# GLU tiles of a fused backward pass: an order on VectorE changed, one product a step later, and another buffer for the modulation sums

## The chip, the core and the metric

The kernel runs on one core of one Trainium2 chip. The time is the device time of one execution in microseconds (us). Before the change the median of three runs is 3124.64 us (3122.74 to 3125.85). One more execution was profiled: it took 3127.18 us, and its span, from the first to the last instruction, is 3125.4 us.

## What is computed

A block with layer norms and modulation (shift, scale and gate rows made from a condition `c`) holds a recurrent attention and a gated unit (GLU). The kernel returns the output of the block and the gradients for all its inputs. The part that is changed is the GLU, forward and backward, with the layer norm in front of it:

```python
# x is the attention's result with its residual; g, u are 1792 wide, the rest is 512 wide
h = layernorm(x) * (1 + cb) + sb
g = h @ w_gate;  u = h @ w_up
hh = sigmoid(g) * u
b = hh @ w_down
out = x + gb * b
# reference: jax.vjp of the whole block; the gradients of sb, cb, gb and ga are sums over all 2048 rows
```

## The kernel before

The stage (`phase3`) treats 2048 rows in 16 tiles of 128 rows. Each tile goes through seven steps, `s0` to `s6`, and `run_pipeline` works one step of seven different tiles in each iteration, the deepest step first. In iteration `it` the tile `j` of step `k` is `it - k`, so there are 22 iterations: the first ones fill the pipeline, iterations 6 to 15 hold all seven steps, and from iteration 16 on `s0` is gone, from 18 on `s2`, and so on.

- `s0` (layer norm): `t0 = a_rows*ga`, `x1 = t0 + x0`, statistics, `rstd` and `db = dout*gb` on GpSimd (called POOL in the profile), `xhf`, `h2a`, `h2`, and the stores of `db` and `h2`.
- `s1`: two DMA transposes on the SyncE queue, into `hdT`.
- `s2`: eight products of 128x448 on TensorE, gate and up in turn, taken out of PSUM by ScalarE as `sg` and `u`. Then `hh = sg*u` on VectorE, its store, and `umh = u - hh` on POOL.
- `s3`: four products of 128x448 (`dp`). VectorE multiplies each by `sg` into a quarter of `du` (L1064), and then makes `dg = du*umh` (L1065). POOL issues the stores DUROWS and DGROWS.
- `s4`: `hhT @ w_down` into one PSUM tile, copied to `b_bf` by ScalarE. VectorE makes `t1 = b_bf*gb` (L1084), POOL `o_sb = t1 + x1` (L1086) and the store of the output (L1087). VectorE makes `pr = dout*b_bf` (L1089), a product that `s6` sums over the rows.
- `s5`: 28 products into one PSUM tile (`hp`, L1099). ScalarE copies it (`dh2b`), VectorE makes `dxh` (L1106), `pr2` (L1109), `junk` with a sum (L1112), `bb`, `cc`, `ta`, and `dx1` (L1124). Then come the store DX1ROWS, `da = dx1*ga` on VectorE (L1127), the store DAROWS, and `pr3 = dx1*a_rows` on POOL (L1130, `pr_ga` in the profile).
- `s6`: four products with ones sum `pr3`, `dh2b`, `pr2` and `pr` into `acc_ps`, and `da` is transposed on TensorE.

PSUM tiles of the stage come from one pool of five (`psM`). In one iteration they are taken in the order `hp`, `bp`, four `dp`, then gate and up eight times. So the first up product can only be written when the first quarter of `du` has read the first `dp`, the second gate product when the second quarter has read its `dp`, and so on.

The order of each engine's instructions is fixed when the kernel is built, by a scheduler that works from the program's order and its own estimate of times; each engine then works its list strictly in order and waits for semaphores. On VectorE a full iteration has this order before the change: `hh` of the iteration before, `dxh`, `pr2`, `junk`, `bb`, `cc`, `ta`, `dx1`, `t1`, `da`, `pr`, four `du`, `t0`, `dg`, `x1`, statistics, `xhf`, `h2a`, `h2`, `hh`. On POOL: `umh`, DX1ROWS, `pr_ga`, DAROWS, `o_sb`, output store, DUROWS, DGROWS, `rstd`, `db`, DBROWS, H2ROWS, HHROWS, `umh`.

After the loop the four modulation sums are copied from `acc_ps` to a tile `accs` of the stage's pool `sbp` (L1184), and POOL issues four small DMAs from it to DMOD (L1186). Then the pools of the stage close. The next part computes the gradients of the weights (L1164, L1234) and, mixed in, turns attention weights for the following stage: TensorE transposes into two PSUM tiles `wtp`, and VectorE (two of three) or ScalarE (one of three) copies them to `WoT`, which lies where the closed pools were. The ScalarE queue also issues a 2 MB load of the rows `h2` into the buffer `Wk` (L1222), from element 8192 to 16384 of each partition; in the instruction list it stands ahead of ScalarE's first copy to `WoT`.

Of the kernel before, what the change touches and what calls it, by code (L numbers as in the profile page):

```python
# [7 lines left out]
BF16 = mybir.dt.bfloat16  # L8
F32 = mybir.dt.float32
AF = mybir.ActivationFunctionType  # L10
ALU = mybir.AluOpType
# [29 lines left out]
class K:  # L41
# [879 lines left out]
    def phase3(self):  # L921
        nc, tc, cfg, io = self.nc, self.tc, self.cfg, self.io
        D, DC, F, FC, NT, T = cfg.D, cfg.DC, cfg.F, cfg.FC, cfg.NT, cfg.T
# [4 lines left out]
        out_rows = io["out_0"].rearrange("o s d -> (o s) d")  # L928
        nseg = 128 // T
        d = self.dram  # L930
        with ExitStack() as ctx:
# [4 lines left out]
            sbp = ctx.enter_context(tc.tile_pool(name="p3s", bufs=2, reuse_waits="tile"))  # L936
            w_gate, w_up, w_down, w_gateT, w_upT = self.w_gate, self.w_up, self.w_down, self.w_gateT, self.w_upT
            w_downT = wtp.tile([128, DC, F], BF16, name="w_downT")
            ga_bc, sb_bc, cb1_bc, gb_bc = (self.bcs[i] for i in (2, 3, 4, 5))
# [8 lines left out]
            def mm():  # L948
                return psM.tile([128, 512], F32, name="mm", tag="m")
# [78 lines left out]
            def s2(j, st):  # L1028
# [19 lines left out]
                st.update(sg=sg, hh=hh, umh=umh)  # L1048
                return st

            def s3(j, st):
                r0, r1 = j * 128, (j + 1) * 128
                sg, umh, hdT = st["sg"], st["umh"], st["hdT"]
                hhT = sbp.tile([128, FC, 128], BF16, name="hhT", bufs=1)
                nc.sync.dma_start(hhT[:], st["hh"][:], transpose=True)
                du = sbp.tile([128, F], BF16, name="du", bufs=2)
                dg = sbp.tile([128, F], BF16, name="dg", bufs=2)
                for ch in range(NCH):
                    sl = slice(ch * CH, (ch + 1) * CH)
                    dp = mm()  # L1060
                    for c in range(DC):
                        nc.tensor.matmul(dp[:, 0:CH], lhsT=hdT[:, DC + c, :], rhs=w_downT[:, c, sl],
                                         start=(c == 0), stop=(c == DC - 1))
                    nc.vector.tensor_tensor(du[:, sl], dp[:, 0:CH], sg[:, sl], op=ALU.mult)  # L1064
                nc.vector.tensor_tensor(dg[:], du[:], umh[:], op=ALU.mult)  # L1065
                nc.gpsimd.dma_start(self.DUROWS[r0:r1, :], du[:])
                nc.gpsimd.dma_start(self.DGROWS[r0:r1, :], dg[:])
                st.update(hhT=hhT, du=du, dg=dg)
                return st

            def s4(j, st):
                r0, r1 = j * 128, (j + 1) * 128
                hhT = st["hhT"]
                bp = mm()
                for fc in range(FC):
                    nc.tensor.matmul(bp[:], lhsT=hhT[:, fc, :], rhs=w_down[:, fc, :], start=(fc == 0), stop=(fc == FC - 1))
                duT = sbp.tile([128, FC, 128], BF16, name="duT", bufs=1)
                dgT = sbp.tile([128, FC, 128], BF16, name="dgT", bufs=1)
                nc.sync.dma_start(duT[:], st["du"][:], transpose=True)
                nc.sync.dma_start(dgT[:], st["dg"][:], transpose=True)  # L1080
                b_bf = sbp.tile([128, D], BF16, name="b_bf", bufs=2)
                nc.scalar.activation(b_bf[:], bp[:], AF.Copy)
                t1 = sbp.tile([128, D], F32, name="t1", tag="f32tmp", bufs=5)
                nc.vector.tensor_tensor(t1[:], b_bf[:], gb_bc[:], op=ALU.mult)  # L1084
                o_sb = sbp.tile([128, D], BF16, name="o_sb", bufs=2)
                nc.gpsimd.tensor_tensor(o_sb[:], t1[:], st["x1"][:], op=ALU.add)  # L1086
                nc.gpsimd.dma_start(out_rows[r0:r1, :], o_sb[:])  # L1087
                pr = sbp.tile([128, D], BF16, name="pr_gb", bufs=3)
                nc.vector.tensor_tensor(pr[:], st["dout"][:], b_bf[:], op=ALU.mult)  # L1089
                st.update(duT=duT, dgT=dgT, pr=pr)  # L1090
                return st

            def s5(j, st):
                r0, r1 = j * 128, (j + 1) * 128
                hp = mm()
                n = 0
                for (xT, wT) in ((st["duT"], w_upT), (st["dgT"], w_gateT)):
                    for fc in range(FC):
                        nc.tensor.matmul(hp[:], lhsT=xT[:, fc, :], rhs=wT[:, fc, :], start=(n == 0), stop=(n == 2 * FC - 1))  # L1099
                        n += 1  # L1100
                xh2, rstd, dout, a_rows = st["xh2"], st["rstd"], st["dout"], st["a_rows"]
                dh2b = sbp.tile([128, D], BF16, name="dh2b", bufs=1)
                nc.scalar.activation(dh2b[:], hp[:], AF.Copy)
                dxh = sbp.tile([128, D], F32, name="dxh", tag="f32tmp", bufs=5)
                s1_ = sbp.tile([128, 1], F32, name="s1", bufs=2)
                nc.vector.scalar_tensor_tensor(out=dxh[:], in0=hp[:], scalar=1.0, in1=cb1_bc[:], op0=ALU.mult, op1=ALU.mult,  # L1106
                                               accum_out=s1_[:])
                pr2 = sbp.tile([128, D], BF16, name="pr_cb", bufs=1)
                nc.vector.tensor_tensor(pr2[:], hp[:], xh2[:], op=ALU.mult)  # L1109
                junk = sbp.tile([128, D], F32, name="junk", tag="f32tmp", bufs=5)  # L1110
                s2_ = sbp.tile([128, 1], F32, name="s2", bufs=2)
                nc.vector.scalar_tensor_tensor(out=junk[:], in0=dxh[:], scalar=1.0, in1=xh2[:], op0=ALU.mult, op1=ALU.mult,  # L1112
                                               accum_out=s2_[:])
                bb = sbp.tile([128, 1], F32, name="bb", bufs=2)
                cc = sbp.tile([128, 1], F32, name="cc", bufs=2)
                nc.vector.tensor_scalar(bb[:], s1_[:], rstd[:, 0:1], -1.0 / D, op0=ALU.mult, op1=ALU.mult)
                nc.vector.tensor_scalar(cc[:], s2_[:], rstd[:, 0:1], -1.0 / D, op0=ALU.mult, op1=ALU.mult)
                ta = sbp.tile([128, D], F32, name="ta", tag="f32tmp", bufs=5)
                nc.vector.scalar_tensor_tensor(out=ta[:], in0=dxh[:], scalar=rstd[:, 0:1], in1=dout[:], op0=ALU.mult,
                                               op1=ALU.add)  # L1120
                tb = sbp.tile([128, D], F32, name="tb", tag="f32tmp", bufs=5)
                nc.scalar.activation(tb[:], xh2[:], AF.Identity, scale=cc[:, 0:1], bias=bb[:, 0:1])
                dx1 = sbp.tile([128, D], F32, name="dx1", bufs=1)
                nc.vector.tensor_tensor(dx1[:], ta[:], tb[:], op=ALU.add)  # L1124
                nc.gpsimd.dma_start(self.DX1ROWS[r0:r1, :], dx1[:])
                da = sbp.tile([128, D], BF16, name="da", bufs=2)
                nc.vector.tensor_tensor(da[:], dx1[:], ga_bc[:], op=ALU.mult)  # L1127
                nc.gpsimd.dma_start(self.DAROWS[r0:r1, :], da[:])
                pr3 = sbp.tile([128, D], BF16, name="pr_ga", bufs=1)
                nc.gpsimd.tensor_tensor(pr3[:], dx1[:], a_rows[:], op=ALU.mult)  # L1130
                st.update(dh2b=dh2b, pr2=pr2, pr3=pr3, da=da)
                return st

            def s6(j, st):
# [23 lines left out]
            def load_hr(g):  # L1158
                w = min(384, F - 384 * g)
                (nc.sync if g < 2 else nc.scalar).dma_start(hrs[g][:, :, 0:w], self.HHROWS[:, 384 * g:384 * g + w].rearrange("(j p) f -> p j f", p=128))  # L1160
# [9 lines left out]
            def after(it):  # L1170
                if it == NT + 1:
                    nc.scalar.dma_start(dbr, self.DBROWS[:, :].rearrange("(j p) d -> p j d", p=128))
                elif it == NT + 2:
                    load_hr(0)
                elif NT + 3 <= it < NT + 6:
                    if it == NT + 3:
                        load_hr(1)
                    wd_chunk(it - NT - 3, mm(), sbp.tile([128, D], BF16, name="ot2", tag="db", bufs=2))

            self.run_pipeline(NT, [s0, s1, s2, s3, s4, s5, s6], deepest_first=True, after=after)  # L1180
            ET = mybir.EngineType
            self.pin_behind(i0, self.pinned, [ET.DVE, ET.Activation, ET.Pool])
            accs = sbp.tile([128, D], F32, name="accs", bufs=1)
            nc.vector.tensor_copy(accs[:], acc_ps[:, :])  # L1184
            for i in range(4):
                nc.gpsimd.dma_start(self.DMOD[2 + i:3 + i, :], accs[32 * i:32 * i + 1, :])  # L1186
# [906 lines left out]
```

The softmax here doesn't subtract the row's maximum and nothing guards it: scores larger than these inputs give would overflow.

## Time and profile before

| what | value |
|---|---|
| median of three runs | 3124.64 us |
| profiled execution / its span | 3127.18 us / 3125.4 us |
| TensorE busy, all of the span | 3004.2 us (96%) |
| VectorE, ScalarE, POOL busy | 1616.2, 1264.6, 1473.0 us |
| GLU tiles, iterations 4 to 21 | about 1060 to 1380 us of the span |
| one iteration, first six full ones | 20.13 us |
| one iteration, the next ones | 19.70 us |
| TensorE's idle time at L1043 in the stage | 16.3 us in 15 waits |
| mean granted TensorE clock | 0.989 |

The lengths of an iteration are the distances of the `da` product from one iteration to the next: it starts at 1085.45, 1105.58, 1125.71, 1145.84, 1165.97, 1186.11, 1206.24 us and then every 19.70 us. The same product takes 2.07 us in the first six of these and 0.69 us in the other ones. The page's times are those of one execution; a wait is put down to the event that came last.

### The profile page before, as it was taken

Reading aid. Unit: us, or ns where it says so; the run is one execution under the profiler, and the core shown is the slowest. Engines: PE = TensorE matmul, PEld = TensorE weight load, DVE = VectorE, ACT = ScalarE, POOL = GpSimd, SP = SyncE. Lnnn points to the kernel's source line nnn. Section 1 sums busy time; section 2 is a strip of 40 time slices with the busy share of each in tenths; the row PEclk is TensorE's granted clock in tenths of the full one; section 3 lists DMA queues with packets and bytes.
Section 4 is the critical chain, followed back from the end, with each engine's and each line's share of the span. In section 5 each row is a group of like instructions: output and inputs, shape, how many; then the busy total and the mean of one; then the engine's idle time right before and its main releaser. Section 6 shows DMA issues by size and latency. Waiting matters only on the chain.

```text
span 3125.4 us, 106126 instructions
## 1 busy us (share of the span) xinstructions
PE 3004.2 (96%) x43769; PEld 1838.1 (59%) x43845; DVE 1616.2 (52%) x3738; ACT 1264.6 (40%) x3053; POOL 1473.0 (47%) x2974
## 2 busy tenths in 40 slices
PE   5999999999998799989989999999999999999999
PEld 3666666666665444445567777777777754455454
DVE  4556656655654777733255555555655542322321
ACT  2555555555554433322155555555555530110111
POOL 3666666666665466531144444444444432233322
PEclk8999999999999899999999999999999999999999
DMA  8887788788787798898589999999999998666674
GB/s 295 214 214 199 205 214 212 204 207 213 205 207 237 177 214 219 202 267 271 185 218 244 240 248 242 244 243 248 244 239 244 243 270 285 201 202 213 196 234 147
DMA packets 844665, 703.54 MB, mean 225 GB/s; under 512 B 543794, under 2 KB 716370, under 8 KB 843796
## 3 DMA queue, kind: packets, MB, share of 16 engines
q1 hardware_dynamic: 714404, 486.69, 62.2%
q0 software_dynamic: 59120, 148.64, 14.6%
q10 hardware_dynamic: 70656, 61.41, 6.3%
q8 instruction: 345, 5.65, 0.8%
q14 instruction: 140, 1.15, 0.1%
HBM read 294.93 MB, written 276.35 MB: 183 GB/s over the span
## 4 chain that ended last, share of the span: by engine, by line
PE 50%; issue 4%; DMA 2%; POOL 1%; DVE 0%; SPq 0%; ACT 0%; POOLq 0%; DVEq 0%
PE gps L1885 10%; PE dh_ps L216 8%; PE g_ps L1547 6%; PE pass_ps L256 5%; PE gps5o L1899 4%; PE dhq_ps L224 4%; PE gps L1234 3%; PE dh_tps L216 3%; PE dp_ps L1526 2%; PE tps L1459 2%; PE dp_ps L1534 1%; PE turn_ps L1413 1%; PE dh_ft L321 1%; PE gps L1164 1%; PE wtp L1300 1%
## 5 line engine op out<-in xcount | busy, mean ns | idle before, releaser
L1885 PE MATMUL gps<-rows,hrows 128*128 128x512 bf16 (+2 forms) x2124 | 415.6, 355 | 1.9
L1885 PEld LDWEIGHTS <-hrows 128*128 128x128 bf16 x2160 | 211.2, 98 | 204.6
L256 PEld LDWEIGHTS <-hT 128*32 128x32 bf16 x6144 | 158.2, 97 | 161.3 <-issue 1.9
L1591 POOL COPY dOst<-RAd 96x512 bf16<-96x512 bf16 x128 | 75.4, 613 | 311.3 <-DVE RAd L63 311.1
L1889 POOL DMA_DIRECT2D out_dram<-ot x108 | 81.4, 754 | 258.6 <-DVE ot L63 132.3
L63 DVE CAST ot<-gps 128x512 bf16<-128x512 f32 (+3 forms) x76 | 48.1, 633 | 284.9 <-PE gps L1885 191.6
L875 POOL TENSOR_TENSOR Pst<-Pst,rden 120x1408 bf16<-120x1408 bf16 x63 | 159.6, 2533 | 57.4 <-issue 38.9
L61 ACT ACTIVATE ot<-gps 128x512 bf16<-128x512 f32 (+3 forms) x75 | 41.3, 551 | 356.2 <-PE gps L1885 225.3
L61 ACT ACTIVATE dVT<-g_ps 128x512 bf16<-128x512 f32 (+1 forms) x192 | 109.3, 569 | 95.9 <-PE g_ps L1547 95.5
L63 DVE CAST RA0v<-pass_ps 128x512 bf16<-128x512 f32 x128 | 88.5, 692 | 89.5 <-PE pass_ps L256 86.2
L216 PE MATMUL dh_ps<-WvT,dVT 128*32 128x512 bf16 x2048 | 133.4, 380 | 0.0
L256 PE MATMUL pass_ps<-Wv,hT 128*32 128x512 bf16 x2048 | 133.3, 380 | 0.0
L1899 PE MATMUL gps5o<-WoT,rows 128*128 128x512 bf16 x580 | 127.8, 379 | 1.0 <-DMA rows<-OSR 0.3
L224 PE MATMUL at_ps<-Wo,OT 128*32 128x256 bf16 x4096 | 125.0, 275 | 0.1
L256 PE MATMUL pass_ps<-Wk,hT 128*32 128x512 bf16 x2048 | 123.3, 383 | 1.5 <-ACT hT L865 1.1
L1536 DVE SCALAR_TENSOR_TENSOR dS<-dp_ps,Pst_l 128x512 bf16<-128x512 f32 (+1 forms) x192 | 112.0, 639 | 22.8 <-PE dp_ps L1534 22.8
L256 PE MATMUL pass_ps<-WoT,dyT 128*32 128x256 bf16 (+1 forms) x3072 | 122.4, 308 | 0.9 <-ACT dyT L1665 0.9
L224 PE MATMUL dhq_ps<-WqT,dQT 128*32 128x256 bf16 x4096 | 122.9, 273 | 0.0
L216 PE MATMUL dh_ps<-WkT,dKT 128*32 128x512 bf16 x2048 | 122.3, 380 | 0.0
L256 PE MATMUL pass_ps<-Wq,hT 128*32 128x512 bf16 x2048 | 121.6, 379 | 0.0
L224 PEld LDWEIGHTS <-dQT 128*32 128x32 bf16 x4096 | 109.6, 97 | 15.9
L709 ACT ACTIVATE ET<-st_ps 128x480 bf16<-128x480 f32 (+1 forms) x192 | 96.1, 535 | 42.6 <-ACT qT L61 34.7
(419 smaller groups left out, 7164.5 us busy)
## 6 DMA issues: line engine op xcount, KB each, us to landing
OSR<-Ost SPq DMA_DIRECT2D x64, 352.0 KB
OT<-OT SPq DMA_DIRECT2D x64, 352.0 KB
VT<-VTr SPq DMA_DIRECT2D x64, 352.0 KB
PS<-Pst SPq DMA_DIRECT2D x64, 352.0 KB
OT_l<-OT SPq DMA_DIRECT2D x64, 352.0 KB
Pst_l<-PS SPq DMA_DIRECT2D x64, 352.0 KB
VT_l<-VT SPq DMA_DIRECT2D x64, 352.0 KB
DVR<-rows_x POOLq DMA_DIRECT2D x64, 352.0 KB, 6.4
```

The costliest lines, as they stand in the source:

```text
L61: return nc.scalar.activation(out, in_, AF.Copy)
L63: return nc.vector.tensor_copy(out, in_)
L216: self.nc.tensor.matmul(ps[32 * j:32 * j + 32, :], lhsT=lhsT, rhs=w, start=(n < 4), stop=(n >= total - 4), tile_position=(0, 32 * j))
L224: nc.tensor.matmul(ps[32 * j:32 * j + 32, :], lhsT=x[k], rhs=w[k][:, 256 * d:256 * d + 256], start=(n == 0), stop=(n == total - 1), tile_p ...
L256: self.nc.tensor.matmul(ps[32 * j:32 * j + 32, :], lhsT=lhs(c), rhs=rhs, start=(c == 0), stop=(c == DC - 1), tile_position=(0, 32 * j))
L709: nc.scalar.activation(part3(ET, pi)[:, 0:n, 0:120], st_ps[:, 0:n, 0:120], AF.Exp, scale=cfg.scale)
L875: nc.gpsimd.tensor_tensor(Pst[0:120, :, :], Pst[0:120, :, :], rden[:, :].unsqueeze(2).to_broadcast([120, G, 128]), op=ALU.mult)
L1234: nc.tensor.matmul(ps[:], lhsT=h2r[:, j, c * 128:(c + 1) * 128], rhs=xr[:, j, :], start=(j == 0), stop=(j == NT - 1))
L1536: nc.vector.scalar_tensor_tensor(out=part3(dS, pi), in0=ps[:, 0:n, :], scalar=cfg.scale, in1=part3(Pst, pi), op0=ALU.mult, op1=ALU.mult)
L1547: nc.tensor.matmul(ps[:, j, :], lhsT=lh[:, g * GW:(g + 1) * GW], rhs=rh[:, g * GW:(g + 1) * GW], start=True, stop=True)
L1885: nc.tensor.matmul(ps[:, 0:ng * E], lhsT=hrows[:, tp_, c * 128:(c + 1) * 128], rhs=rows[:, tp_, 0:ng * E], start=(tp_ == 0), stop=(tp_ == ...
L1899: nc.tensor.matmul(pss[gg][:], lhsT=src[0][:, src[1], gg * E:(gg + 1) * E], rhs=dyrows[:, tp_, :], start=(tp_ == order[0]), stop=(tp_ == o ...
```

## The change

`s3` runs all its VectorE work on `dp` first and then calls `flush`, which works off a list of things put aside: the output's product with its sum and store (from `s4`), and the product `da` with its store (from `s5`). `after` calls `flush` too, for iterations without `s3`. The product `pr` is written in `s5` and not in `s4`, with two buffers instead of three. The sums go to a region of the weight buffer `Wk` (elements 14336 to 15360 of each partition) and not to a tile of the stage's pool.

```diff
+            late = []
+            def flush():
+                while late:
+                    late.pop(0)()
 ...
             def s3(j, st):
 ...
                     nc.vector.tensor_tensor(du[:, sl], dp[:, 0:CH], sg[:, sl], op=ALU.mult)
+                flush()
                 nc.vector.tensor_tensor(dg[:], du[:], umh[:], op=ALU.mult)
 ...
             def s4(j, st):
 ...
-                t1 = sbp.tile([128, D], F32, name="t1", tag="f32tmp", bufs=5)
-                nc.vector.tensor_tensor(t1[:], b_bf[:], gb_bc[:], op=ALU.mult)
-                o_sb = sbp.tile([128, D], BF16, name="o_sb", bufs=2)
-                nc.gpsimd.tensor_tensor(o_sb[:], t1[:], st["x1"][:], op=ALU.add)
-                nc.gpsimd.dma_start(out_rows[r0:r1, :], o_sb[:])
-                pr = sbp.tile([128, D], BF16, name="pr_gb", bufs=3)
-                nc.vector.tensor_tensor(pr[:], st["dout"][:], b_bf[:], op=ALU.mult)
-                st.update(duT=duT, dgT=dgT, pr=pr)
+                def out():
+                    t1 = sbp.tile([128, D], F32, name="t1", tag="f32tmp", bufs=5)
+                    nc.vector.tensor_tensor(t1[:], b_bf[:], gb_bc[:], op=ALU.mult)
+                    o_sb = sbp.tile([128, D], BF16, name="o_sb", bufs=2)
+                    nc.gpsimd.tensor_tensor(o_sb[:], t1[:], st["x1"][:], op=ALU.add)
+                    nc.gpsimd.dma_start(out_rows[r0:r1, :], o_sb[:])
+                late.append(out)
+                st.update(duT=duT, dgT=dgT, b_bf=b_bf)
 ...
             def s5(j, st):
 ...
+                pr = sbp.tile([128, D], BF16, name="pr_gb", bufs=2)
+                nc.vector.tensor_tensor(pr[:], dout[:], st["b_bf"][:], op=ALU.mult)
 ...
-                nc.vector.tensor_tensor(da[:], dx1[:], ga_bc[:], op=ALU.mult)
-                nc.gpsimd.dma_start(self.DAROWS[r0:r1, :], da[:])
+                def out():
+                    nc.vector.tensor_tensor(da[:], dx1[:], ga_bc[:], op=ALU.mult)
+                    nc.gpsimd.dma_start(self.DAROWS[r0:r1, :], da[:])
+                late.append(out)
 ...
+            later = after
+            def after(it):
+                flush()
+                later(it)
 ...
-            accs = sbp.tile([128, D], F32, name="accs", bufs=1)
+            accs = self.flat(self.Wk, 2 * DC * F, 2 * D, F32)
```

The scheduler turns this into the following order of a full iteration. VectorE: `hh` of the iteration before, `dxh`, `pr2`, `junk`, `bb`, `cc`, `ta`, `dx1`, `du`, `du`, `da`, `du`, `du`, `t1`, `dg`, `t0`, `pr`, `x1`, and the rest as before. The product `pr` is brought forward over the end of the iteration, so that it stands in the same iteration as before, only later. POOL: `umh`, DX1ROWS, `pr_ga`, DAROWS, DUROWS, `o_sb`, DGROWS, output store, `rstd`, and the rest as before. TensorE's, ScalarE's and SyncE's orders within the stage stay. In iteration 4 VectorE's order is `t1`, `du`, `du`, `t0`, `du`, `du`, `x1`, `dg`, where it was `t1`, `pr`, four `du`, `t0`, `dg`, `x1`. In the last iteration POOL's `pr_ga` comes ahead of DAROWS. After the loop, VectorE's first copy to `WoT` no longer waits for the DMAs to DMOD, and the load of the `h2` rows on ScalarE's queue now waits for all four of them.

More of the change, by code (lines that the diff above doesn't have):

```diff
@@ L1126, in s5 @@
                 da = sbp.tile([128, D], BF16, name="da", bufs=2)
-                nc.vector.tensor_tensor(da[:], dx1[:], ga_bc[:], op=ALU.mult)
-                nc.gpsimd.dma_start(self.DAROWS[r0:r1, :], da[:])
+                def out():
+                    nc.vector.tensor_tensor(da[:], dx1[:], ga_bc[:], op=ALU.mult)
+                    nc.gpsimd.dma_start(self.DAROWS[r0:r1, :], da[:])
+                late.append(out)
                 pr3 = sbp.tile([128, D], BF16, name="pr_ga", bufs=1)
                 nc.gpsimd.tensor_tensor(pr3[:], dx1[:], a_rows[:], op=ALU.mult)
-                st.update(dh2b=dh2b, pr2=pr2, pr3=pr3, da=da)
+                st.update(dh2b=dh2b, pr2=pr2, pr3=pr3, da=da, pr=pr)
                 return st
```

## The prediction

> **What bounds the kernel now.** First the totals: TensorE is busy for 96% of the span. So I looked for the places in the stage where TensorE stands still, in the list of waits between 1040 and 1385 us, and then read what happens there from the timeline.
>
> ```profile
> PE mm L1043 <- DVE du L1064: 16.3, 15, 3.4
> DVE dxh L1106 <- ACT dh2b L1103: 57.1, 16, 5.7
> ```
>
> The first line is all that TensorE loses inside the loop: 15 waits for `du`, 16.3 us. The second seems to say that VectorE has some 3.5 us to spare in each iteration. The timeline of one iteration shows both, and why the second is deceptive:
>
> ```profile
> 1179.21 3.59 POOL L1047 TENSOR_TENSOR umh<-u,hh 128x1792 bf16<-128x1792 bf16 x1
> 1183.02 0.68 DVE L1112 SCALAR_TENSOR_TENSOR junk<-dxh,xh 128x512 f32<-128x512 f32 x1
> 1186.11 2.07 DVE L1127 TENSOR_TENSOR da<-dx,Wv 128x512 bf16<-128x512 f32 x1
> 1186.45 1.17 POOL L1130 TENSOR_TENSOR pr_ga<-dx,Wv 128x512 bf16<-128x512 f32 x1
> 1188.10 0.41 DVE L1089 TENSOR_TENSOR pr_gb<-Wq,b_bf 128x512 bf16<-128x512 bf16 x1
> 1188.44 2.21 DVE L1064 TENSOR_TENSOR du<-mm,sg 128x448 bf16<-128x448 f32 x4
> 1189.10 0.92 PE L1043 MATMUL mm<-Wk,hdT 128*128 128x448 bf16 x4 [1.17 <-DVE du L1064]
> ```
>
> TensorE waits 1.17 us because `du` stands behind `t1`, `da` and `pr`. `da` needs 2.07 us here and 0.69 us where it gets by: it stood still until POOL's `pr_ga` ended (1187.62) and was done 0.56 later. VectorE products of two SBUF tiles and POOL's products shut each other out. `du` (one input in PSUM) is never slowed: 0.60 to 0.61 us in all 64. Look at `junk`: it starts 0.22 after `umh` ends. It has two SBUF inputs, so it could not have started sooner. Two more places show the size of it:
>
> ```profile
> 1061.58 5.31 DVE L1089 TENSOR_TENSOR pr_gb<-Wv,b_bf 128x512 bf16<-128x512 bf16 x1
> 1061.80 3.58 POOL L1047 TENSOR_TENSOR umh<-u,hh 128x1792 bf16<-128x1792 bf16 x1
> 1065.33 1.26 POOL L1086 TENSOR_TENSOR o_sb<-t,x 128x512 bf16<-128x512 f32 x1
> ...
> L1926 DVE SCALAR_TENSOR_TENSOR dx_junk<-dx_dxh,xh x16: 681/1524/1531, 2608.4 to 2992.7; 128x512 f32<-128x512 f32 x16
> ```
>
> `pr` (0.41 alone) sat out `umh` and `o_sb` together; in the last stage the same form as `junk` takes 1.52 instead of 0.68 where POOL is ahead. Behind the loop, the chain of waits and the timeline show the sums' way out:
>
> ```profile
> 1382.11 6.04 DMA DMOD<-accs
> ...
> 1388.71 0.76 DVE L63 COPY WoT<-wtp 128x512 bf16<-128x512 bf16 x2 [4.44 <-DMA DMOD<-accs]
> 1389.19 1.01 PE L1313 MATMUL wtp<-ident,stage 128*128 128x128 bf16 x8 [4.34 <-DVE WoT L63]
> ```
>
> TensorE waits 4.34 us for a copy that waits for four 2 KB DMAs, and then runs at half clock until 1396 (eight transposes 1.01 us, where they take 0.61 at 1395.84).
>
> **The change, part by part.** I take the profiled execution as it is; its span is 0.8 above the median of the runs, so I take the difference off 3124.64.
>
> *Full iterations.* Time 0 is 1185.51, where the operation after `dx1` starts. Now two `du` go first (0.53 each), and `da` comes to 1.06. `pr_ga` runs from 0.94 to 2.11, so `da` is always late and the next operation starts at 2.59 (as before: 0.48 after `pr_ga`). Two `du`: 3.65. `t1` 0.60: `dg` starts at 4.25. On POOL, DAROWS waits for `da`, DUROWS for the last `du` (3.73, plus the 0.29 that every store waits after its tile): 4.03 to 4.58. `o_sb` waits for `t1`, whose record ends at 4.34. So `dg` has the port first, until 5.33; `o_sb`, waiting, gets it next, as `pr_ga` did ahead of `pr` in the ten faster iterations (there `da` ended at 1206.93, `pr_ga` 1.01 later), and ends at about 6.4. `t0` stands behind it, the next operation starts at 6.9, `pr` takes 0.34, and `x1` starts at 7.24. Before, it was 1192.17 - 1185.51 = 6.66, or 6.23 in the faster iterations. From `x1` to the end of `hh` nothing changes (6.32): 13.56. `umh` ends 4.45 after `hh` (1198.49 to 1202.94): 18.01. If `junk` is there by then it ends 0.55 later, 18.56, and from the end of `junk` to time 0 it is 1.81 (1183.70 to 1185.51). This ring of VectorE and POOL is 20.37 us long. Before it was 12.98 + 4.45 + 0.55 + 1.81 = 19.79 with the slow `da` and some 19.4 with the fast one, below the 20.13 and 19.70 that ran, so it did not show. Is `junk` there? The first up product starts 0.1 after the first `du`, at 0.7; `hp` ends 12.2 later (1189.10 to 1201.30), `dxh` 0.63 after that, `junk` at 14.7: well ahead of 18.0. So the ring decides. TensorE alone would need 20.13 - 1.17 = 18.96, and goes on waiting for `du`, 1.4 us each time. Eleven such iterations (5 to 15): 11 x 20.37 = 224.1 against 6 x 20.13 + 5 x 19.70 = 219.3: **+4.8**.
>
> *Way out.* In iteration 16 the first `du` comes 2.5 sooner after `dx1` (at 0 and not behind `t1`, `da` and `pr`): **-2.5**. `s0` is gone there, `hh` comes early, `umh` is over before `junk`, so iteration 17 is TensorE's alone: **-0.7** (19.70 - 18.96).
>
> *Iteration 4.* The 3.4 us wait (first `du` behind the 5.31) and 1.5 us of slow clock after it (four products in 1.65 and 1.70, for 0.92 each). Now two `du` go ahead of the blocked operation, which is `t0`; the third comes at 1067.1, so TensorE waits 2.2, two product groups later. That is 2.6 less if a wait of 2.2 keeps the clock (the 1.97 us wait at 1413 kept it, 3.39 and 3.74 did not). `umh` then meets `junk` in the next iteration, 0.4: **-2.2**; bounds -1.2 (clock lost anyhow) and -3.
>
> *The sums.* VectorE's copy is free of DMOD, but the load of the `h2` rows now lies over the sums' new home, so it waits for the same four DMAs on ScalarE's queue. Queued behind it is ScalarE's first copy to `WoT`, for which the fifth transposed tile waits (two PSUM tiles). `pr_ga` ahead of DAROWS ends TensorE's 0.75 wait at 1379.15, and puts DMOD's last issue at about 1381.3; 5.1 to 6.0 to land: 1387; eight waits are read off, and the copy ends near 1388.5. By then TensorE has done the third and fourth tile, which before ended at 1390.85: 2.3 gained, and 2.3 more of slow clock if a gap of some 2.4 us keeps it. But the weights' loads bound the next part: one takes 9.3 us (1403.92 to 1413.25) and TensorE waits 2.0 for it; whoever comes sooner waits longer, and the 2 MB load, 6 us later, now runs beside them. I take **-3.0**, nearer the row of the wait than that of the clock; bounds 0 (all given back at 1413) and -7.9 (4.34, 2.8 of clock, 0.75).
>
> `pr` costs nothing by moving (0.34 in either place; two buffers are enough, since it is read in the next iteration). DGROWS and the output store only change places; all eight stores of an iteration have a step's time to land.
>
> Sum: -2.2 + 4.8 - 2.5 - 0.7 - 3.0 = -3.6, that is **3121.0 us**.
>
> The Trainium skill ("SBUF — State Buffer", section "Who interferes with whom") states the port rule seen above, and says that whoever starts first has the pair for its whole instruction. The rows differ: six times `da` starts 0.34 ahead of `pr_ga` and loses, ten times, with the same lead, it wins. By the page `dg` wins with its lead of 0.33; by the six rows `o_sb` would, and the sum would be the 3126 of the second rival. I side with `dg` because `pr_ga`'s input had long been there.
>
> **The rivals.** *TensorE-bound:* `junk` does not stop for `umh`, the 16.3 us go, with 1.5 of clock and 3.0 at the end: 3103.8. For it: the 3.4 us before `dxh`. Against: `dx_junk`'s 1.52.
>
> *`o_sb` before `dg`* (the slower side). If POOL takes the port before 4.25, `dg` ends at 6.8, then `t0`, `pr`, and `x1` starts at 7.7: the ring is 20.82, 5.0 more in eleven iterations: **3126.0**. It decides from a `t1` that ends 0.1 sooner or a `dg` that starts 0.1 later. For it: POOL's lost 0.3 in the six slow `da`. Against: `t1`.
>
> *The end gives all:* the load of the rows waits, but ScalarE's copy costs TensorE nothing, and the weights are there: -7.9, so 3116.1. Against: the 2.0 us wait at 1413. The opposite, an end worth nothing, gives 3124.0 and is in my own case.
>
> **The numbers.** Forecast 0.53, `o_sb` first 0.23, the whole end 0.18, TensorE-bound 0.06. No change means within 0.2%, 6.2 us, what a measurement of this kernel can tell: 3118.4 to 3130.9. Faster: 0.06, most of 0.18, a tenth of the rest: 0.30. Slower: a fourth of the second rival and a little of the forecast, where two of its bounds come together: 0.13. Same: 0.57. Range: down past the whole end with a good iteration 4 (3111), up past `o_sb` first with an end worth nothing (3129). The likeliest case alone: 3117 to 3125.
>
> **What would show it.** Right: iterations of about 20.4 us from 5 to 15, `junk` near 1.5 us or longer and ending 0.55 after `umh`, `da` always slow, TensorE still waiting some 1.4 us at the first up product, one gap at the `WoT` copies of 2 to 3 us, now behind ScalarE. Wrong: a `junk` of 0.68 and no wait for `du` (first rival), a `dg` of 2 us or more (second), no gap at `WoT` (third), or a longer wait at the weights' loads than 2.0.

## The result, and the profile after

In runs beside each other the changed kernel takes 3125.69 us (median of 4, 3123.23 to 3126.6) and the kernel before 3125.24 us (median of 4): a ratio of 1.0001, 95% interval 0.9984 to 1.0018. That is no change that can be measured. The profiled execution took 3126.6 us, with a span of 3124.8 us. By the traces, changes of 0.6 to 5 us lie under it that nearly cancel.

The waits of the changed kernel in the stage (engine, line, what it waited for: us in all, times, longest):

```profile
PE mm L1043 <- DVE du L1070: 13.0, 14, 2.1
PE mm L1039 <- ACT b_bf L1089: 3.7, 11, 0.3
DVE dxh L1117 <- ACT dh2b L1114: 28.1, 16, 5.7
ACT tb L1133 <- DVE cc L1128: 60.6, 16, 4.4
```

TensorE waits for `du` 13.0 us in place of 16.3, and has a new wait for `b_bf`. VectorE's idle time ahead of `dxh` has halved (57.1 before), and ScalarE's wait for `cc`, the number that follows `junk`, has grown (36.4 before). VectorE's spare time has moved into a stall. The timeline of one iteration shows where:

```profile
1183.22 0.92 PE L1039 MATMUL mm<-Wk,hdT 128*128 128x448 bf16 x4 [0.34 <-ACT b_bf L1089]
1183.32 1.15 DVE L1070 TENSOR_TENSOR du<-mm,sg 128x448 bf16<-128x448 f32 x2
1184.27 1.16 POOL L1145 TENSOR_TENSOR pr_ga<-dx,Wv 128x512 bf16<-128x512 f32 x1
1184.39 1.60 DVE L1140 TENSOR_TENSOR da<-dx,Wv 128x512 bf16<-128x512 f32 x1
1186.58 0.92 PE L1043 MATMUL mm<-Wk,hdT 128*128 128x448 bf16 x4 [0.91 <-DVE du L1070]
1187.58 1.08 DVE L1072 TENSOR_TENSOR dg<-du,umh 128x1792 bf16<-128x1792 bf16 x1
1187.91 1.88 POOL L1095 TENSOR_TENSOR o_sb<-t,x 128x512 bf16<-128x512 f32 x1
1188.58 1.75 DVE L993 TENSOR_TENSOR t<-Wv 128x512 f32<-128x512 bf16 x1
1197.77 3.59 POOL L1047 TENSOR_TENSOR umh<-u,hh 128x1792 bf16<-128x1792 bf16 x1
1199.11 2.81 DVE L1123 SCALAR_TENSOR_TENSOR junk<-dxh,xh 128x512 f32<-128x512 f32 x1
```

`junk` took 0.68 before and takes 2.81 now: `umh` runs until 1201.36, and `junk` ends 0.56 later, at 1201.92. `da` stands behind `pr_ga` and takes 1.60; `dg` has the port ahead of `o_sb` and takes 1.08; `t0` stands behind `o_sb`. The first two `du` are early, and still TensorE waits 0.91 us for the third, which stands behind `da`, and 0.34 for `b_bf`, which stands behind `tb` on ScalarE, which waits for `cc`.

Executions of one kernel scatter by 6 to 9 us to either side of the median (24 of the kernel before, in one set, took 3120.5 to 3135.1, with a median of 3126.6). So I also cut each trace at marks that every kernel has: the start of the first `hh`, `dx1` of iterations 5, 16 and 20, and the first product with `WoT` in the next stage (the group `pass_ps<-WoT,dyT`). Lengths in us, with the median from that kernel's runs and its ratio to the kernel before in the same set:

| kernel | `hh` to it. 5 | 5 to 16 | 16 to 20 | 20 to `WoT` | sum | median, ratio (95%) |
|---|---|---|---|---|---|---|
| before | 39.31 | 219.31 | 72.12 | 186.8 | 517.6 | |
| after | 37.43 | 224.41 | 70.56 | 186.2 | 518.6 | 3125.69, 1.0001 (0.9984 to 1.0018) |
| order_only | 38.24 | 224.47 | 70.07 | 188.9 | 521.7 | 3128.32, 1.0005 (0.9996 to 1.0013) |
| sums_only | 39.27 | 219.32 | 69.81 | 186.9 | 515.3 | 3125.81, 0.9995 (0.9986 to 1.0003) |
| umh_vectore_new | 33.31 | 206.84 | 71.72 | 187.5 | 499.4 | 3105.64, 0.9936 (0.9922 to 0.9950) |
| umh_vectore_old | 33.31 | 218.82 | 68.54 | 186.3 | 507.0 | 3116.35, 0.9969 (0.9956 to 0.9981) |
| junk_psum | 38.24 | 212.29 | 71.28 | 184.6 | 506.4 | 3119.07, 0.9977 (0.9967 to 0.9987) |
| umh_split | 37.85 | 225.97 | 70.51 | 193.1 | 527.4 | 3130.29, 1.0017 (1.0007 to 1.0026) |
| h2_late | 33.31 | 206.85 | 71.13 | 183.4 | 494.7 | 3104.74, 0.9941 (0.9927 to 0.9954) |
| umh_vectore_new_pool_sums | 33.31 | 206.85 | 71.13 | 186.4 | 497.7 | 3106.73, 0.9945 (0.9932 to 0.9958) |
| rows_load_scalar | 37.45 | 224.54 | 75.18 | 188.6 | 525.8 | 3132.04, 1.0017 (1.0008 to 1.0026) |
| all_three | 33.31 | 217.01 | 74.33 | 187.0 | 511.7 | 3107.89, 0.9934 (0.9920 to 0.9947) |

Read the columns first: the eleven iterations repeat to within 0.13 us wherever the loop is the same (all_three is told of below). The last stretch scatters by several us, and the one from iteration 16 to 20 by 2.3: before and sums_only have the same order of instructions there and take 72.12 and 69.81.

### The profile page after: what moved, and what is told of

The parts are those of the page before. It is cut to its first block, busy times and chain, and to the rows that moved or that the text cites. A ratio compares the mean times of both kernels' runs of the same rounds, so it can differ in the third digit from the quotient of the medians.

```text
span 3124.8 us, 106211 instructions
## 1 busy us (share of the span) xinstructions
PE 3009.3 (96%) x43845; PEld 1838.9 (59%) x43845; DVE 1650.7 (53%) x3738; ACT 1264.3 (40%) x3053; POOL 1479.8 (47%) x2974
## 4 chain that ended last, share of the span: by engine, by line
PE 50%; issue 4%; DMA 3%; POOL 1%; DVE 0%; SPq 0%; ACT 0%; POOLq 0%; ACTq 0%; DVEq 0%
PE gps L1906 9%; PE dh_ps L216 8%; PE g_ps L1568 6%; PE pass_ps L256 4%; PE gps5o L1920 4%; PE dhq_ps L224 4%; PE gps L1255 3%; PE dh_tps L216 3%; PE dp_ps L1547 2%; PE tps L1480 2%; PE dp_ps L1555 1%; PE turn_ps L1434 1%; PE dh_ft L321 1%; POOL out_dram L1910 1%; PE wtp L1321 1%
## 5 line engine op out<-in xcount | busy, mean ns | idle before, releaser
L311 DVE TENSOR_TENSOR dST<-dh_ps,dST 128x512 bf16<-128x512 f32 x64 | 44.3, 692 | 131.2 <-ACT dST L310 131.2
```

## The experiments

### The two halves of the change

order_only is the changed kernel with the sums back in the stage's pool; sums_only is the kernel before with the sums in `Wk` (the same two lines the other way round).

```diff
-            accs = self.flat(self.Wk, 2 * DC * F, 2 * D, F32)
+            accs = sbp.tile([128, D], F32, name="accs", bufs=1)
```

> The changed order with the sums back in a tile of the stage's pool. By the prediction's steps (-2.2 in iteration 4, +4.8 in the ring, -3.2 on the way out) it is 0.6 us faster than before. By the two traces (iteration 4 -1.9, eleven iterations +5.1, way out -1.6) it is 1.7 us slower. Iterations 5 to 15 should be 20.40 us apart, junk 2.8 us, as in the changed kernel; the gap at the first copy to WoT should be back near 4.3 us, since that copy then waits for DMOD again. If the sums' new home had anything to do with the iterations, they would differ from 20.40.

> The old order with the sums in Wk. By the prediction's step it is 3.0 us faster than before. By the trace of the changed kernel it is worth 0.4 to 0.6: the copy to WoT then waits for the last store DAOT, which lands only 0.6 to 0.8 us before the DMOD stores did, and what is gained there is lost again at the weights' loads at about 1398 and 1413 us. Iterations stay at 20.13 and 19.70.

The iterations are 20.40 us with the order alone and 20.13 and 19.70 with the sums alone: the loop is the order's work and none of the sums'. The order costs 5.16 in the eleven iterations; ahead of them the trace has 1.07 less and behind them 2.05 less, the last within that stretch's scatter. By medians, each against the kernel before in its set, order_only is 1.7 us slower and sums_only 0.8 faster; neither is clear of noise.

In sums_only the copy to `WoT` comes much sooner. The timeline (in brackets the wait, and what the profile takes for its cause):

```profile
1380.99 1.67 SPq L1266 DMA_DIRECT2D daq<-DAOT  x2
1381.59 0.76 DVE L63 COPY WoT<-wtp 128x512 bf16<-128x512 bf16 x2 [1.62 <-DMA DMOD<-Wk]
1382.06 0.72 PE L1313 MATMUL wtp<-ident,stage 128*128 128x128 bf16 x8 [1.51 <-DVE WoT L63]
1385.10 0.38 PE L1313 MATMUL wtp<-ident,Wv 128*128 128x128 bf16 x4 [1.20 <-ACT WoT L61]
```

TensorE loses 1.51 + 1.20 here in place of 4.34, and its transposes nearly keep their speed: eight in 0.72 us and four in 0.38, where the kernel before took 1.01 for eight. By the terms of my sum that is worth 4.4 (1.6 of the gap, 2.8 of the clock). But the stretch to the first product with `WoT` takes 186.9 us, against 186.8 before. What was gained went into the waits for weights: 2.5 us at the loads of `A_Wo`, 1.0 at `A_Wv` and 2.0 at `A_Wk`, where the kernel before has 2.0, 0.6 and none.

The same copy in the changed kernel:

```profile
1386.84 0.92 SPq L1287 DMA_DIRECT2D daq<-DAOT  x2
1387.42 0.37 ACTq L1243 DMA_DIRECT2D Wk<-H2ROWS  x1
1387.43 0.76 DVE L63 COPY WoT<-wtp 128x512 bf16<-128x512 bf16 x2 [3.44 <-DMA Wv<-HHROWS]
1387.91 1.01 PE L1334 MATMUL wtp<-ident,stage 128*128 128x128 bf16 x8 [3.34 <-DVE WoT L63]
```

Neither cause in brackets can be right: in the instruction list the copy waits neither for the DMOD stores nor for the load of the `hh` rows, but it does wait for the last DAOT store (of `da`, transposed), whose source `daT` lies where `WoT` comes to lie. SyncE's load `daq` waits for that store too (in the trace the two share a semaphore), so its issue tells when it landed. With the sums in `Wk` the copy starts 0.6 us after `daq` in every kernel (after, sums_only, umh_vectore_new, junk_psum, umh_split, h2_late and the two below); with the sums in the pool it starts 3.6, 2.1, 2.6 and 1.3 us after it (before, order_only, umh_vectore_old, umh_vectore_new_pool_sums). So the new home does take the DMOD stores off this wait, and the next in line is a store that lands 0.7 to 3.0 us sooner.

### The ring

umh_vectore_new is the changed kernel, and umh_vectore_old the kernel before, with one word changed:

```diff
-                nc.gpsimd.tensor_tensor(umh[:], u[:], hh[:], op=ALU.subtract)
+                nc.vector.tensor_tensor(umh[:], u[:], hh[:], op=ALU.subtract)
```

> The changed kernel with umh on VectorE right after hh (about 1.05 us there, by bytes against dg's 1.08). If the ring through umh and the blocked junk is what holds the changed kernel at 20.40, junk falls to 0.68, an iteration to TensorE's own 18.96 to 19.1, the waits for du and b_bf go, and the kernel is 15 to 19 us faster than before (3106 to 3110). If TensorE's waits come from the blocked da and t0 alone, junk is short but an iteration stays above 20, and the time within 3 us of before.

> The kernel before with umh on VectorE right after hh. If the old order holds the iteration by itself (du behind t1, da and pr), the iterations stay at 20.13 and 19.70, TensorE's 1.17 and 0.74 us waits for du stay, and only the 5.31 us product in iteration 4 is gained: 3 to 5 us faster (3120 to 3122). If umh was the limit of the old kernel too, the iterations fall to 19 us here as well, and the new order is worth nothing of itself.

The first: an iteration of 18.80 to 18.81 us, and 0.9936 of the time before. VectorE's timeline of it:

```profile
1183.68 1.09 DVE L1047 TENSOR_TENSOR umh<-u,hh 128x1792 bf16<-128x1792 bf16 x1
1186.38 0.68 DVE L1123 SCALAR_TENSOR_TENSOR junk<-dxh,xh 128x512 f32<-128x512 f32 x1
1189.93 1.59 DVE L1140 TENSOR_TENSOR da<-dx,Wv 128x512 bf16<-128x512 f32 x1
```

`umh` takes 1.09 us on VectorE (3.59 on POOL), `junk` is back at 0.68, and from 1040 to 1320 TensorE waits for nothing at all. `da` is as slow as in the changed kernel, so it was not `da` that held the loop.

The second: TensorE's waits in the stage hardly move,

```profile
PE mm L1043 <- DVE du L1064: 11.8, 13, 1.2
```

16.3 less the 3.4 of iteration 4 and some 1 us ahead of it, and the iterations stay at 20.11 and 19.70. So the old order holds itself, as expected. My 3 to 5 us were too few: it is 6.0 faster ahead of iteration 5 (I had counted 3.4 and 1.5) and 3.6 from 16 to 20, where the 3.74 us wait for the `hh` rows is gone (against sums_only, the other trace of the old order, it is 1.3). The two together are the answer on the order: with `umh` on POOL it costs 5.1 in eleven iterations, with `umh` on VectorE it saves 12.0 (218.82 against 206.84).

### Is it the port?

junk_psum lets `junk` read its first input from PSUM:

```diff
-                nc.vector.scalar_tensor_tensor(out=junk[:], in0=dxh[:], scalar=1.0, in1=xh2[:], ...
+                nc.vector.scalar_tensor_tensor(out=junk[:], in0=hp[:], scalar=1.0, in1=xh2[:], ...
```

> The changed kernel with junk reading hp from PSUM in place of dxh from SBUF (the sum then lacks the factor 1+cb). If junk stops only because two SBUF inputs shut VectorE out while POOL's umh runs, junk takes 0.6 to 0.7 us although umh is still running, bb and cc follow, and the next product with two SBUF inputs, ta, stands in its place: it starts about 1 us after junk and ends 0.5 us after umh, 1.5 to 2 us long. The ring then loses bb, cc and ta's own time behind umh (0.12 + 0.13 + 0.68): 19.4 to 19.5 us an iteration, 10 us less in all than the changed kernel, 3114 to 3117. If junk is late for another reason (its semaphore, its accumulating read), it stays at 2.8 and the iterations at 20.40.

```profile
1195.22 3.58 POOL L1047 TENSOR_TENSOR umh<-u,hh 128x1792 bf16<-128x1792 bf16 x1
1196.56 0.68 DVE L1123 SCALAR_TENSOR_TENSOR junk<-mm,xh 128x512 f32<-128x512 f32 x1
1197.41 1.95 DVE L1130 SCALAR_TENSOR_TENSOR ta<-dxh,rstd,Wq 128x512 f32<-128x512 f32 x1
```

`junk` passes in the middle of `umh`, and `ta` stands in its place and ends 0.56 after `umh` (1199.36 and 1198.80). An iteration is 19.30 us. The stall belongs to whichever product with two SBUF inputs comes first, and the ring is 1.10 us shorter: `bb`, `cc` and `ta` no longer follow it, `dx1` no longer waits 0.28 for `tb`, and so `dx1` starts 0.65 after the end of `umh` in place of 1.76. (The median, 3119.07, misses the 3114 to 3117 expected: it is 6 us below the kernel before, less than the trace's 11; its eight runs go from 3113.1 to 3120.9.)

umh_split asks whether a shorter POOL instruction would do:

```diff
-                nc.gpsimd.tensor_tensor(umh[:], u[:], hh[:], op=ALU.subtract)
+                for k in range(2):
+                    hf = slice(k * F // 2, (k + 1) * F // 2)
+                    nc.gpsimd.tensor_tensor(umh[:, hf], u[:, hf], hh[:, hf], op=ALU.subtract)
```

> The changed kernel with umh in two halves on POOL, 1.8 us each. If a waiting VectorE product is let in between two POOL instructions that follow each other, junk waits for the first half at the most: it ends 1.8 us sooner, and an iteration falls to about 19 us (3108 to 3112). If POOL keeps the port from one instruction to the next, as with pr behind umh and o_sb in iteration 4 of the kernel before (5.31 us), junk stays near 2.8 us and an iteration at 20.4 to 20.6.

```profile
1200.33 3.72 POOL L1049 TENSOR_TENSOR umh<-u,hh 128x896 bf16<-128x896 bf16 x2
1201.66 2.95 DVE L1125 SCALAR_TENSOR_TENSOR junk<-dxh,xh 128x512 f32<-128x512 f32 x1
```

It would not. `junk` waits out both halves, and since they take 3.72 together, an iteration is 20.55.

### The stretch behind the loop

h2_late (on umh_vectore_new) pins the 2 MB load behind the last load of `hh` rows; umh_vectore_new_pool_sums is umh_vectore_new with the sums in the pool.

```diff
                 elif fc == 8:
+                    i4 = len(self.traced())
                     load_hr(4)
                 elif fc == 9:
                     nc.scalar.dma_start(h2r, ...)
+                    self.pin(i4, [mybir.EngineType.Activation])
```

> umh on VectorE in the changed kernel, and the 2 MB load of the h2 rows put behind the last load of hh rows on ScalarE's queue (about 1391 us in place of 1365; its first reader is at 1425). If the stretch after the loop is bound by the weights' loads because the 2 MB load shares the DMA engines with them, TensorE's waits of 2.4 and 1.4 us at the weights' loads fall below 1, and the stretch from the last dx1 to the first product with WoT, 187.5 us with umh on VectorE alone (186.2 to 188.9 in the five other runs), falls to 183 to 185: 3101 to 3104. If each weight load is bound by its own slot and its reader, the stretch stays at 186 to 188 and the time at 3105.

> umh on VectorE in the changed kernel, with the sums back in a tile of the stage's pool. By the prediction's step the sums' home is worth 3.0 us, so this is 3.0 slower than with the sums in Wk (3108.6 against 3105.6). By the six traces, in which the stretch after the last dx1 is 186.2 to 188.9 us with either home, it is worth nothing: 3104 to 3107, with a gap of 4 us or more at the first copy to WoT all the same. Iterations at 18.80.

The load is issued at 1397.64, and the stretch is 183.4 us, the shortest of all. The waits at the loads of `A_Wo` fall from 2.6 to 0.7, those at `A_Wv` rise from 1.4 to 2.4. Each against the kernel before in its own set, h2_late is 20.4 us faster and umh_vectore_new 21.0, and the intervals overlap. The trace speaks, weakly, for the 2 MB load as a part of the bound (junk_psum has 184.6 us with the load in its old place), the times neither for nor against it. With the sums in the pool, TensorE's gap at the copy is 3.97 in place of 2.47 and the stretch 186.4 in place of 187.5. Over the first ten rows of the table the gap goes from 1.96 to 4.44 and the stretch from 183.4 to 193.1, and the longest stretch (umh_split) belongs to a gap of 3.24: the gap's length can't be seen in it. Three pairs of kernels differ in the sums' home alone. By medians, each taken against the kernel before in its own set, the new home is better by 1.3 (after, order_only), 0.8 (sums_only, before) and 2.5 us (umh_vectore_new, umh_vectore_new_pool_sums), all within the scatter. Between nothing and 3 us its worth stays open.

rows_load_scalar (on the changed kernel) and all_three (on h2_late) issue the first load of `hh` rows from ScalarE's queue, since TensorE waits 4.7 us for it.

```diff
-                (nc.sync if g < 2 else nc.scalar).dma_start(hrs[g][:, :, 0:w], ...
+                (nc.sync if g == 1 else nc.scalar).dma_start(hrs[g][:, :, 0:w], ...
```

> The changed kernel with the first load of the hh rows (1.5 MB into Wk) issued by ScalarE and no longer by SyncE, where it stands behind three transposes. In the changed kernel it is issued at 1347.8, and TensorE waits 4.7 us for it in iteration 19 and then runs its first 16 products in 5.14 us (3.63 where the wait was 3.11). On ScalarE it stands behind tb of iteration 18, so it is issued at about 1342.5. If what the way out gains is given back at this load, the wait falls below 1, the products take 3.6, and from dx1 of iteration 16 to that of iteration 20 it is 64 to 66 us in place of 70.6: the kernel is 4 to 6 us faster than the changed one. If the load is bound by its 1.5 MB and by what else is on the DMA engines, the wait only moves, and the gain is below 2.

> The changed kernel with umh on VectorE, the first load of the hh rows on ScalarE, and the load of the h2 rows behind the last load of hh rows. With umh on VectorE alone it was 3105.6 with a wait of 4.4 us at the hh rows. If the two loads add to it as they should (4 to 6 for the first, 1 to 3 for the second): 3097 to 3101. If the wait at the hh rows is made up for elsewhere: 3103 to 3106.

Both miss. In rows_load_scalar the load is issued at 1343.50, but the transpose `hhT`, which is issued next, takes 8.55 us, and TensorE waits 6.13 us for it:

```profile
1346.48 8.55 SPq L1061 DMA_TRANSPOSE hhT<-hh  x1
1361.47 6.08 PE L1083 MATMUL mm<-Wv,hhT 128*128 128x512 bf16 x14 [6.13 <-DMA hhT<-hh]
```

In the changed kernel it was the other way about:

```profile
1344.57 2.98 SPq L1061 DMA_TRANSPOSE hhT<-hh  x1
1347.77 0.40 SPq L1175 DMA_DIRECT2D Wk<-HHROWS  x1
```

The DMA engines are busy throughout there (a share of 1.11 from 1343 to 1360 us of the changed kernel), and the products with `hhT` come first: in these two traces what the load gained, the transpose lost.

## Why the prediction was right, and where it was not

The time is 3125.7 where 3121.0 was forecast, inside the range and just outside the 3117 to 3125 of the likeliest case; "no change" had the highest chance. By the table's cuts the change costs 1.0 us (518.6 less 517.6) where my sum said -3.6. The ring came as forecast; the three gains against it (-2.2, -3.2, -3.0) came out as -1.9, -1.6 and -0.6, all too small, so that the time stayed in the range by its width.

*The ring, +4.8: right.* 20.37 us was the forecast, 20.40 the measurement, +5.1 over eleven iterations. Each link came as worked out: `da` always late, `dg` ahead of `o_sb`, `t0` behind `o_sb`, `pr` 0.41, `junk` ending 0.56 after `umh`. That it is this ring, and this port, is shown by umh_vectore_new and junk_psum. `junk` takes 2.8 us, longer than "near 1.5".

*Where TensorE waits: wrong in place, right in size.* I put 1.4 us at the first up product. It is 0.91 at the second, whose PSUM tile the third `du` frees, and 0.34 at the first gate product: 1.25. I had not followed the late `cc` through `tb` to `b_bf` on ScalarE's list. As the ring sets the period, the wait had to turn up somewhere; umh_vectore_new shows TensorE's own period as 18.80, not 18.96.

*Way out, -3.2: half.* Iterations 17 and 18 come 1.4 and 1.0 sooner (18.33 and 18.81 against 19.76). Of these 2.4 us 0.8 are lost again up to iteration 20, where the wait for the `hh` rows is 4.68 in place of 3.74: -1.6 in all. The step ended its account at iteration 17 and named nothing that could be late next; it was this load. Its wait stood in the list of waits of the kernel before, so the wait for `du` was not all that TensorE lost inside the loop:

```profile
PE mm L1164 <- DMA Wk<-HHROWS: 3.7, 1, 3.7
```

The -1.6 is not clear of scatter either: in sums_only, with the old order, the load cost 3.11 us and the stretch took 69.81, less than the changed kernel's 70.56. What repeats is the 2.4 of iterations 17 and 18 (order_only, junk_psum and umh_split have it too).

*Iteration 4, -2.2: right, with luck in the clock.* From `hh` to iteration 5 it is 1.9 less. `t0` stands 4.51 us, the wait is 2.14 (2.2 forecast), and the products after it run at full speed:

```profile
1060.98 4.51 DVE L993 TENSOR_TENSOR t<-Wv 128x512 f32<-128x512 bf16 x1
1066.08 0.92 PE L1043 MATMUL mm<-Wk,hdT 128*128 128x448 bf16 x4 [2.14 <-DVE du L1070]
```

In order_only the same stretch gained 1.07: the same wait of 2.14 us is followed there by slow products, 1.45, 1.70 and 1.38 us for the 0.92 of the changed kernel.

```profile
1066.59 1.45 PE L1043 MATMUL mm<-Wk,hdT 128*128 128x448 bf16 x4 [2.14 <-DVE du L1070]
```

junk_psum (2.14) is slow as well, umh_split (2.28) and rows_load_scalar (2.15) are not. So a wait of this length keeps the clock in some executions only, and the bound of -1.2 was as good a forecast as -2.2.

*The sums, -3.0: the step that failed.* It said that VectorE's copy, free of DMOD, would come at once, and that ScalarE's copy behind the 2 MB load would be the new gap. In fact the copy waits for the DAOT store, and in the changed kernel that landed only in time for 1387.43: the gap fell from 4.34 to 3.34, the eight transposes behind it still took 1.01 us, and the waits for the loads of `A_Wo` and `A_Wv` rose from 2.6 to 4.0. The kernel before shows the store already: `daq` is issued at 1385.05, 3.66 ahead of the copy; the step had no term for it. And where the gap did close, in sums_only, the stretch stayed at 186.9. The measured worth by the traces is -0.6 (after), +0.1 (sums_only) and +1.1 (umh_vectore_new against umh_vectore_new_pool_sums), all within what this stretch scatters; by the medians it is 0.8 to 2.5 us better. So the mechanism was wrong, and the size stays open. The traces are nearer the bound that I named and left: "all given back at 1413".

*The rivals.* TensorE-bound: `junk` did stop. `o_sb` ahead of `dg`: `dg` was 1.08 in every iteration. The whole end: no.

## What to carry to other kernels

Before moving work on the engine that seems to be late, look for the longest ring through it and the engine that it shares a resource with. Here the order was a good one (12 us in eleven iterations), but only after 3.6 us of POOL work had been taken off the port; one word then did what the new order alone could not. When a wait on many semaphores is to be made shorter, look for the second to last of them as well, and then for what bounds the stretch: a gap that closes in front of a queue of loads may give nothing, as in the trace of sums_only. The version to keep is the changed kernel with `umh` on VectorE (0.9936, 0.9922 to 0.9950); h2_late and all_three can't be told from it.

## What was not expected of the hardware

POOL can keep the shared port from one instruction to the next. In umh_split a VectorE product that had been waiting for some 0.5 us when the first half ended (half of 3.72 after 1200.33, against 1201.66) was not let in between two POOL instructions, and in iteration 4 of the kernel before `pr` sat out `umh` and `o_sb`. In both places the second POOL instruction's record starts 0.05 to 0.06 us before the first one's ends. The Trainium skill ("SBUF — State Buffer", section "Who interferes with whom") speaks of the pair being held for the whole instruction, by whoever issues first; in these two places it was held through two instructions. Nor do the starts in the profile decide who gets it: with a lead of 0.33 to 0.35 us over `pr_ga`, `da` of the kernel before lost six times and won nine (the prediction counts ten, but in the tenth the lead was 1.54).

One SBUF input can be enough to be shut out. `xhf` reads one tile and two scalars for each partition, and takes 0.55 us in the one place where it is nearly alone and 1.38 in the others, where POOL's `db` starts 0.05 to 0.07 us ahead of it (kernel before; durations in ns: least, median, most):

```profile
L1011 DVE TENSOR_SCALAR xhf<-x,mv,rstd x16: 546/1380/1384, 1020.9 to 1293.2; 128x512 f32<-128x512 f32 x16
```

The same section lists this operation among those that can take both ports in a fast mode and then contend with GpSimd. The row agrees that it is shut out; which mode it ran in no run here shows.

The next limit may be the DMA engines. From 1090 to 1290 us (columns: length, busy time of TensorE, its weight loads, VectorE, ScalarE and POOL, clock, DMA share, GB/s) of before, umh_vectore_new and all_three:

```profile
1090.00:1290.00 200.00, 189.93 (x976) 90.87 (x985) 154.32 (x262) 73.08 (x132) 123.41 (x132) 1.00 0.90 217
```

```profile
1090.00:1290.00 200.00, 199.47 (x1033) 96.50 (x1041) 183.50 (x288) 77.73 (x140) 96.92 (x128) 1.00 1.00 228
```

```profile
1090.00:1290.00 200.00, 192.55 (x990) 91.26 (x989) 173.34 (x273) 73.82 (x133) 91.73 (x122) 0.99 1.02 214
```

With TensorE's waits gone, the DMA share rises from 0.90 to 1.00, and TensorE is busy for 199.5 of 200 us. all_three has the same loop, but in its profiled execution, the slowest of its five (3120.75), the transposes `hhT`, `dgT` and `duT` came late in four iterations and TensorE waited 7.5 us for them. Its eleven iterations took 10.2 us more than h2_late's (217.01 against 206.85), most of the 12.9 by which that execution is above the median. Whether the slow executions of the other fast versions have the same cause, no trace shows.
